# A fixed order of operations on four engines for a top-k attention and SoLU kernel, with two scratch buffers for its counting passes

## The chip, the cores and the metric

The kernel runs on one core of a Trainium2 chip. A core has a matrix engine (PE, whose weight loads are listed as PEld), a vector engine (DVE), a scalar engine (ACT), a general engine (POOL) and a synchronisation engine (SP, used here for DMA). Each takes its instructions from its own queue in order; semaphores let one wait for another. The metric is the device time of one execution in microseconds.

## The reference

Attention keeps, in each row of scores, the 32 largest; what follows is a feed-forward block whose activation is SoLU with a layer norm. All is float32 in the result; the weights come in as float64.

```python
# q, k, v: (8, 8, 576, 64) = batch, heads, sequence, head_dim; top_k = 32
scores = scale * np.matmul(q, k.transpose(0, 1, 3, 2))
kth = np.partition(scores, -top_k, axis=-1)[..., -top_k:-top_k + 1]
scores = np.where(scores >= kth, scores, -1000000000.0)
scores = scores - np.max(scores, axis=-1, keepdims=True)
attn = np.exp(scores)
attn = attn / (np.sum(attn, axis=-1, keepdims=True) + 1e-09)
x = np.matmul(attn, v)                 # then (B, H, S, D) -> (4608 tokens, 512)
...
h = x @ w_in                           # 512 -> 1024
e = np.exp(h - h_max)
solu = h * (e / (np.sum(e, axis=-1, keepdims=True) + 1e-09))
ln = (solu - mu) / np.sqrt(var + 1e-06) * g_ln
return (ln @ w_out).astype(np.float32) # 1024 -> 512
```

## The kernel before, in words

The attention works on 32 pairs of heads (8 batches, 4 pairs each). A pair has nine tiles of 128 rows by 576 scores: four tiles of 128 rows for each of two heads, and one that holds the last 64 rows of both. The k-th value of a row isn't found by sorting but by counting and correcting a threshold. For a pair `i` the steps are, by function:

- `load_qk`, `load_v`: DMAs on SP. q and k have one buffer each.
- `prep`: PE transposes q and k into PSUM tiles of the tag `tp` (two of them), ACT copies them; PE makes moments of k and multiplies q with them; DVE (L669, L673) and POOL (L675, L678, a power; L691) turn that into a first threshold `t0` and its step (`ta`, `tb`).
- `scores(i, t)`: for t = 0 to 4, PE writes two score tiles (PSUM tag `big`, two of two banks each; L715). ACT copies each to SBUF (`X`, L723). DVE counts the scores over `t0` (L728); what it writes besides the count goes to a scratch tile `junkv` with one buffer.
- `second`: four short DVE passes (L736 to L743) make the second threshold `t1`.
- `count1`: ACT counts with Sign (L751), scratch `junka` with one buffer. `third`: DVE makes the third threshold `t2` (L760 to L768). `count2`: ACT counts again (L783) and keeps the signs `sg` (nine buffers).
- `nearest`: DVE makes distances to the threshold (`side`'s pass L795, then L801 for each tile) and takes the eight smallest (L805, MAX8). `kth`: seven short DVE passes (L818 to L833) pick the k-th value.
- `exps`: ACT's exponentials of three tiles at a time (L812).
- `softmax`: DVE masks the exponentials and sums them (L843); POOL inverts three sums at a time (L849, and a power, L852) and multiplies the three tiles (L855).
- `transpose_p`, `transpose_last`: PE transposes the probabilities into the `tp` tiles (L872, L890, L886), ACT copies them out (L879, L892, L887). `attn_v`: PE multiplies them with v in three parts (L912), ACT copies the result (L918, L920).

When the four pairs of a batch are done, its tokens are queued in groups of 128: four for a batch, and one more for every second batch, 36 in all. `mm1` (PE, L933), `solu_ln` (DVE L943 to L954, ACT L946 and L958, POOL L959 to L964) and `mm2` (eight transposes L974, copies L977, 16 matmuls L980, copy L985, store from ACT's DMA queue L987). Weights are converted from float64 in 16 chunks (`weights_step`, lines 31 to 52, on DVE and POOL).

The Python code calls these functions from `slot(i)`, which mixes the first half of pair `i` with the second half of pair `i - 1`; `pop()` takes the next piece of token or weight work from a list. This order is a priority only: the framework's scheduler, with its own model of costs, decides in which order each engine gets the instructions, and interleaves them freely where data and buffers allow.

Of the kernel before, what the change touches and what calls it, by code (L numbers as in the profile page):

```python
# [443 lines left out]
def fast_path(  # L444
# [165 lines left out]
    def prep(i):  # L610

        d = st[i]
        qkT = p2.tile([P, 2, S], F32, tag="qkT", name="qkT")

        mom = p2.tile([P, D + 1], F32, tag="mom", name="mom")
        tails = ps_tp.tile([P, NM, P], F32, tag="tp", name="tp_t")
        for n, nm in enumerate("qk"):
            nc.tensor.transpose(
                tails[:, 0, n * ST : (n + 1) * ST], d[nm + "t"].rearrange("p h d -> p (h d)"),
                ident[0:ST, 0:ST],  # L620
            )
        nc.scalar.copy(
            out=qkT[:, :, SM:S],
            in_=tails[:, 0, 0 : 2 * ST].rearrange("p (n s) -> p n s", n=2),
        )
        for n, nm in enumerate("qk"):
            tp = ps_tp.tile([P, NM, P], F32, tag="tp", name="tp_qk")
            for c in range(NM):
                nc.tensor.transpose(
                    tp[:, c, :], d[nm][:, 2 * c : 2 * c + 2, :].rearrange("p h d -> p (h d)"),  # L630
                    ident,
                )
            if nm == "q":
                nc.scalar.copy(out=qkT[:, n, 0:SM], in_=tp.rearrange("p c s -> p (c s)"))
            else:
                nc.scalar.activation(
                    out=qkT[:, n, 0:SM], in_=tp.rearrange("p c s -> p (c s)"), func=AF.Copy,
                    accum_out=mom[:, D : D + 1],
                )
        d["qkT"] = qkT  # L640
        tm = ps_tp.tile([P, NM * P], F32, tag="tp", name="tp_m")
        for c in range(NM + 1):
# [6 lines left out]
        nc.scalar.copy(out=mom[:, 0:D], in_=tm[:, 0:D])  # L649

        ty = ps_tp.tile([P, NM * P], F32, tag="tp", name="tp_y")
        tt = ps_o.tile([P, 512], F32, tag="o", name="y_t")
        ys = [
            ty[:, 0 : NM * (D + 1)].rearrange("p (t e) -> p t e", e=D + 1),
            tm[:, 2 * D : 2 * D + NM * (D + 1)].rearrange("p (t e) -> p t e", e=D + 1),
            tt[:, 0 : D + 1].unsqueeze(1),
        ]
        for t in range(NM + 1):
            for h in range(2):
                hd = slice(h * D, (h + 1) * D)  # L660
                qs = slice(SM, S) if t == NM else slice(t * P, (t + 1) * P)
                nc.tensor.matmul(
                    out=ys[2][h * ST : (h + 1) * ST, 0, :] if t == NM else ys[h][:, t, :],
                    lhsT=trunc(qkT[hd, 0, qs]), rhs=trunc(mom[hd, :]), start=True, stop=True,
                )
        ys = [(slice(h, 2 * NM, 2), ys[h]) for h in range(2)] + [(slice(2 * NM, NT), ys[2])]
        yq = p2.tile([P, NT, D], F32, tag="w", name="yq")
        for js, y in ys:
            nc.vector.tensor_tensor(  # L669
                out=yq[:, js, :], in0=y[:, :, 0:D], in1=d["q"][:, js, :], op=ALU.mult  # L670
            )
        ss = small.tile([P, NT], F32, tag="ss", name="ss")
        nc.vector.tensor_reduce(out=ss, in_=yq, axis=AX.X, op=ALU.add)  # L673
        zs = small.tile([P, NT], F32, tag="zs", name="zs")
        nc.gpsimd.tensor_scalar(  # L675
            out=zs, in0=ss, scalar1=(Z0 * scale) ** 2 / S, scalar2=0.0, op0=ALU.mult, op1=ALU.add
        )
        nc.gpsimd.tensor_tensor(out=zs, in0=zs, in1=phalf.broadcast_to([P, NT]), op=ALU.pow)  # L678
        t0 = small.tile([P, NT], F32, tag="t0", name="t0")
        for js, y in ys:  # L680
            nc.vector.scalar_tensor_tensor(
                out=t0[:, js], in0=y[:, :, D], scalar=scale / SM, in1=zs[:, js],
                op0=ALU.mult, op1=ALU.add,
            )

        ta = small.tile([P, NT], F32, tag="ta", name="ta")
        nc.vector.scalar_tensor_tensor(
            out=ta, in0=zs, scalar=GAIN, in1=t0, op0=ALU.mult, op1=ALU.add
        )
        tb = small.tile([P, NT], F32, tag="tb", name="tb")  # L690
        nc.gpsimd.tensor_scalar(  # L691
            out=tb, in0=zs, scalar1=-63.0 * GAIN, scalar2=1.0, op0=ALU.mult, op1=ALU.mult
        )
        d["t0"], d["ta"], d["tb"] = t0, ta, tb
# [4 lines left out]
    def scores(i, t):  # L699
# [19 lines left out]
        for j, s in zip(js, big):  # L719
            if j % 3 == 0:  # L720
                d["X"][j // 3] = p6.tile([P, 3, S], F32, tag="X", name="X")
            x = x_of(i, j)
            nc.scalar.activation(  # L723
                out=x.rearrange("p (a s) -> p a s", a=2), in_=s[:, :, 0:SH],
                func=AF.Copy, scale=scale,
            )
            junk = p1.tile([P, S], BF16, tag="junkv", name="junkv")
            nc.vector.tensor_scalar(  # L728
                out=junk, in0=x, scalar1=d["t0"][:, j : j + 1], scalar2=None,
                op0=ALU.is_ge, op1=ALU.add, accum_out=d["c0"][:, j : j + 1],  # L730
            )
# [16 lines left out]
    def count1(i, j):  # L748
        d = st[i]
        junk = p1.tile([P, S], BF16, tag="junka", name="junka")  # L750
        nc.scalar.activation(  # L751
            out=junk, in_=x_of(i, j), func=AF.Sign, scale=-1.0,
            bias=d["t1"][:, j : j + 1], accum_out=d["n1"][:, j : j + 1],
        )
# [33 lines left out]
    def nearest(i, g):  # L788

# [7 lines left out]
        for j in range(3 * g, 3 * g + 3):  # L799
            w = p2.tile([P, S], F32, tag="w", name="w")  # L800
            nc.vector.scalar_tensor_tensor(  # L801
                out=w, in0=x_of(i, j), scalar=d["al"][:, j : j + 1], in1=d.pop(("sg", j)),
                op0=ALU.subtract, op1=ALU.mult,
            )
            nc.vector.max(d["w8"][:, j, :], w)  # L805
# [33 lines left out]
    def softmax(i, g):  # L839
        d = st[i]  # L840
        for j in range(3 * g, 3 * g + 3):
            e = d["E"][g][:, j % 3, :]
            nc.vector.scalar_tensor_tensor(  # L843
                out=e, in0=x_of(i, j), scalar=d["kth"][:, j : j + 1], in1=e,
                op0=ALU.is_ge, op1=ALU.mult, accum_out=den_all[:, i, j : j + 1],
            )
        js = slice(3 * g, 3 * g + 3)
        rden = d["rden"][:, js]
# [4 lines left out]
        for j in range(3 * g, 3 * g + 3):  # L853
            e = d["E"][g][:, j % 3, :]
            nc.gpsimd.tensor_scalar(  # L855
                out=e, in0=e, scalar1=d["rden"][:, j : j + 1], scalar2=1.0,
                op0=ALU.mult, op1=ALU.mult,
            )
# [4 lines left out]
    def transpose_p(i, j):  # L863
        d = st[i]
# [4 lines left out]
        pt = p_of(i, j)  # L869
        tp = ps_tp.tile([P, NM, P], F32, tag="tp", name="tp_p")  # L870
        for c in range(NM):
            nc.tensor.transpose(tp[:, c, :], pt[:, c * P : (c + 1) * P], ident)  # L872
# [6 lines left out]
        nc.scalar.copy(out=dst, in_=tp)  # L879

    def transpose_last(i, part):

        d = st[i]
        tp = ps_tp.tile([P, NM, P], F32, tag="tp", name="tp_pt")
        if part == 2:
            nc.tensor.transpose(tp[0:ST, 0, :], p_of(i, 2 * NM)[:, SM:S], ident)  # L886
            nc.scalar.copy(out=d["PTt"][0:ST, NM, :], in_=tp[0:ST, 0, :])  # L887
            return
        for n in range(4):
            nc.tensor.transpose(tp[0:ST, n, :], p_of(i, 4 * part + n)[:, SM:S], ident)  # L890
# [3 lines left out]
    def attn_v(i, part):  # L894
# [13 lines left out]
        for c in range(NM + 1):  # L908
            ks = P if c < NM else ST
            for h in range(2):  # L910
# [5 lines left out]
                )  # L916
        if part == 1:
            nc.scalar.copy(out=xs["m", b][:, hp, :], in_=d["om"])  # L918
        elif part == 2:
            nc.scalar.copy(  # L920
                out=xs["t", b // 2][:, hp, (b % 2) * ST : (b % 2 + 1) * ST], in_=o
            )
            d.clear()
            if hp == NP - 1:
                queue_batch(b)
# [3 lines left out]
    def mm1(d, x):  # L929
# [10 lines left out]
    def solu_ln(d):  # L940
        h = d["h"]
        nmax = small.tile([P, 1], F32, tag="hmax", name="hmax")
        nc.vector.tensor_reduce(out=nmax, in_=h, axis=AX.X, op=ALU.max, negate=True)  # L943
        e = p1.tile([P, DFF], F32, tag="e", name="e_sb")
        rs = small.tile([P, 1], F32, tag="rs", name="rs")
        nc.scalar.activation(out=e, in_=h, func=AF.Exp, bias=nmax, accum_out=rs)  # L946
        nc.vector.tensor_scalar(out=rs, in0=rs, scalar1=1e-9, scalar2=None, op0=ALU.add)
        nc.vector.reciprocal(rs, rs)
        solu = p2.tile([P, DFF], F32, tag="solu", name="solu")
        nmu = small.tile([P, 1], F32, tag="nmu", name="nmu")  # L950
        nc.vector.scalar_tensor_tensor(
            out=solu, in0=h, scalar=rs, in1=e, op0=ALU.mult, op1=ALU.mult, accum_out=nmu
# [4 lines left out]
        var = small.tile([P, 1], F32, tag="var", name="var")  # L957
        nc.scalar.activation(out=e, in_=solu, func=AF.Square, bias=nmu, accum_out=var)  # L958
# [6 lines left out]
            out=solu, in0=solu, scalar1=nmu, scalar2=rstd, op0=ALU.add, op1=ALU.mult  # L965
        )
        d["ln"] = solu

    def mm2(d, stores):
# [42 lines left out]
    def pop():  # L1012
        if todo:
            todo.pop(0)()
# [116 lines left out]
```

## Time and profile before

| | |
|---|---|
| median of 3 runs | 1764.85 us (1764.52 to 1766.37) |
| the profiled execution | 1766.6 us, span 1764.7 us |
| mean granted PE clock | 0.864 |
| POOL `softmax` waiting for DVE's L843 | 467.6 us in 53 waits |
| ACT `count1` waiting for DVE's `second` | 126.1 us in 32 waits |
| DVE `third` waiting for ACT's `count1` | 134.2 us in 20 waits |

The span runs from the first to the last instruction of the profiled execution. In a group's or timeline's row stand the engine, the line, the operation, the tile written and the tiles read, the shapes and the number of instructions; busy time is given in microseconds. PEclk is the clock that PE was granted, as a share of full speed.

### The profile page before, as it was taken

What the parts mean: (1) busy time and instruction counts of PE and PEld (TensorE: products, weight loads), DVE (VectorE), ACT (ScalarE), POOL (GpSimd) and SP (SyncE); (2) the same over time, 40 slices, a digit from 0 to 9 for tenths busy, and PEclk for the clock granted to TensorE, in tenths of its full rate; (3) what the DMA queues carried; (4) which work ended last, traced back from release to release, by engine and by line L of the source; (5) the groups of instructions that cost most, each with busy time, mean ns of one, the idle gap of its engine ahead of it and who ended that gap; (6) DMA issues with size and microseconds to landing.
All of it is one profiled execution on the core that took longest, in us unless ns stands there. A gap on an engine that the chain in (4) does not pass through costs nothing.

```text
span 1764.7 us, 21722 instructions
## 1 busy us (share of the span) xinstructions
PE 1423.9 (81%) x7043; PEld 782.8 (44%) x7043; DVE 1155.7 (65%) x2816; ACT 1175.2 (67%) x2398; POOL 647.3 (37%) x806
## 2 busy tenths in 40 slices
PE   5364478998889897998789988798789988799696
PEld 3232244454444454544444554445435445345443
DVE  3687876687757567666766677576766856567520
ACT  3656587677866767678767767667776768676521
POOL 5778623342324333142243331333233412433210
PEclk9576688898889888898789988898888988899898
DMA  3211100011001110101101010011001110100000
GB/s 98 73 50 51 33 22 21 21 27 35 14 21 33 28 28 7 27 27 28 26 24 27 20 29 21 21 28 33 22 12 29 28 26 22 27 13 20 1 12 20
DMA packets 101898, 48.68 MB, mean 28 GB/s; under 512 B 86920, under 2 KB 95120, under 8 KB 101776
## 3 DMA queue, kind: packets, MB, share of 16 engines
q1 hardware_dynamic: 96528, 37.77, 8.4%
q10 hardware_dynamic: 5248, 9.44, 1.5%
q8 instruction: 58, 0.95, 0.2%
q14 instruction: 64, 0.52, 0.1%
HBM read 37.75 MB, written 9.44 MB: 27 GB/s over the span
## 4 chain that ended last, share of the span: by engine, by line
PE 38%; DVE 22%; ACT 16%; POOL 15%; issue 7%; DMA 1%; SPq 0%; ACTq 0%; DVEq 0%; POOLq 0%
PE o_ps L980 9%; PE om L912 8%; PE tp_p L872 8%; PE s_ps L715 7%; ACT junka L751 7%; DVE junkv L728 5%; DVE E L843 5%; POOL zs L678 3%; ACT sg L783 3%; DVE w L801 3%; POOL E L855 3%; DVE w L805 2%; POOL solu L964 2%; PE tp_pt L890 2%; PE tp_ln L974 2%
## 5 line engine op out<-in xcount | busy, mean ns | idle before, releaser
L715 PE MATMUL s_ps<-qkT 64*128 64x288 f32 (+1 forms) x1280 | 335.8, 483 | 70.6 <-ACT X L723 50.0
L751 ACT ACTIVATE junka<-X,t 128x576 bf16<-128x576 f32 x288 | 223.0, 774 | 131.2 <-DVE t L743 126.1
L872 PE MATMUL tp_p<-ident,E 128*128 128x128 f32 x1152 | 206.6, 330 | 117.9 <-POOL E L855 59.7
L728 DVE TENSOR_SCALAR_CACHE_REDUCE junkv<-X,t 128x576 bf16<-128x576 f32 x288 | 232.3, 807 | 85.3 <-ACT X L723 78.0
L980 PE MATMUL o_ps<-w_out,lnT 128*128 128x512 f32 x576 | 264.9, 612 | 0.0
L843 DVE SCALAR_TENSOR_TENSOR E<-X,kth,E 128x576 f32<-128x576 f32 x288 | 250.5, 898 | 15.9 <-ACT E L812 13.3
L872 PEld LDWEIGHTS tp_p<-ident,E 128*128 128x128 f32 x1152 | 156.7, 168 | 209.3 <-issue 96.2
L855 POOL TENSOR_SCALAR E<-E,rden 128x576 f32<-128x576 f32 x288 | 243.7, 860 | 9.8
L879 ACT COPY PT<-tp_p 128x512 f32<-128x512 f32 x256 | 143.1, 587 | 151.6 <-PE tp_p L872 149.0
L933 PE MATMUL h_ps<-w_in,xTm 128*128 128x512 f32 x512 | 232.1, 597 | 0.6 <-ACT xTm L918 0.6
L783 ACT ACTIVATE sg<-X,t 128x576 bf16<-128x576 f32 x288 | 220.4, 772 | 16.5 <-DVE t L768 16.2
L715 PEld LDWEIGHTS s_ps<-qkT 64*128 64x128 f32 (+1 forms) x1280 | 161.1, 195 | 157.9 <-ACT X L723 80.7
L801 DVE SCALAR_TENSOR_TENSOR w<-X,al,sg 128x576 f32<-128x576 f32 x288 | 229.5, 823 | 0.6
L849 POOL TENSOR_SCALAR rden<-den_all 128x3 f32<-128x3 f32 x96 | 30.9, 322 | 542.0 <-DVE E L843 467.6
L723 ACT ACTIVATE X<-s_ps 128x576 f32<-128x576 f32 x288 | 178.4, 650 | 68.9 <-PE s_ps L715 56.6
L805 DVE MAX8 w<-w 128x8 f32<-128x576 f32 x288 | 209.8, 750 | 0.0
L980 PEld LDWEIGHTS o_ps<-w_out,lnT 128*128 128x128 f32 x576 | 110.4, 197 | 133.7 <-issue 126.3
L812 ACT ACTIVATE E<-X 128x1728 f32<-128x1728 f32 x96 | 157.6, 1647 | 12.2 <-PE tp_pt L890 12.1
L912 PE MATMUL om<-PT,vm 128*64 128x256 f32 x1024 | 161.7, 454 | 0.1
L933 PEld LDWEIGHTS h_ps<-w_in,xTm 128*128 128x128 f32 x512 | 93.2, 190 | 103.8 <-issue 98.7
L912 PEld LDWEIGHTS om<-PT,vm 128*64 128x64 f32 x1024 | 89.3, 165 | 59.2 <-issue 39.0
L974 PE MATMUL tp_ln<-ident,solu 128*128 128x128 f32 x288 | 52.4, 317 | 63.0 <-POOL solu L964 63.0
(119 smaller groups left out, 1632.0 us busy)
## 6 DMA issues: line engine op xcount, KB each, us to landing
qm<-in_q_dram SPq DMA_DIRECT2D x32, 256.0 KB, 3.4
km<-in_k_dram SPq DMA_DIRECT2D x32, 256.0 KB, 3.3
vm<-in_v_dram SPq DMA_DIRECT2D x32, 256.0 KB, 2.8
out_dram<-osb ACTq DMA_DIRECT2D x32, 256.0 KB, 2.3
w_raw<-in_moe_w_in_dram SPq DMA_DIRECT2D x8, 512.0 KB, 3.8
w_raw<-in_moe_w_out_dram SPq DMA_DIRECT2D x8, 512.0 KB, 3.5
qt<-in_q_dram SPq DMA_DIRECT2D x32, 32.0 KB, 2.2
kt<-in_k_dram SPq DMA_DIRECT2D x32, 32.0 KB, 2.8
```

What stands on the lines that cost most here:

```text
L715: nc.tensor.matmul(out=s[:, half, 0:SH], lhsT=qkT[hd, 0, qs], rhs=qkT[hd, 1, half * SH : (half + 1) * SH], start=True, stop=True,)
L728: nc.vector.tensor_scalar(out=junk, in0=x, scalar1=d["t0"][:, j : j + 1], scalar2=None, op0=ALU.is_ge, op1=ALU.add, accum_out=d["c0"][:, j ...
L751: nc.scalar.activation(out=junk, in_=x_of(i, j), func=AF.Sign, scale=-1.0, bias=d["t1"][:, j : j + 1], accum_out=d["n1"][:, j : j + 1],)
L783: nc.scalar.activation(out=d["sg", j], in_=x_of(i, j), func=AF.Sign, scale=-(1.0 + 2.0**-23), bias=d["t2"][:, j : j + 1], accum_out=d["n2" ...
L801: nc.vector.scalar_tensor_tensor(out=w, in0=x_of(i, j), scalar=d["al"][:, j : j + 1], in1=d.pop(("sg", j)), op0=ALU.subtract, op1=ALU.mult,)
L805: nc.vector.max(d["w8"][:, j, :], w)
L843: nc.vector.scalar_tensor_tensor(out=e, in0=x_of(i, j), scalar=d["kth"][:, j : j + 1], in1=e, op0=ALU.is_ge, op1=ALU.mult, accum_out=den_a ...
L855: nc.gpsimd.tensor_scalar(out=e, in0=e, scalar1=d["rden"][:, j : j + 1], scalar2=1.0, op0=ALU.mult, op1=ALU.mult,)
L872: nc.tensor.transpose(tp[:, c, :], pt[:, c * P : (c + 1) * P], ident)
L912: nc.tensor.matmul(out=o[h * D : (h + 1) * D, :], lhsT=vm[:, h, c, :] if c < NM else vt[:, h, :], rhs=rhs[0:ks, c, :], start=(c == 0), sto ...
L933: nc.tensor.matmul(out=h[:, half, :], lhsT=x[:, c, :], rhs=w_in[:, c, half * 512 : (half + 1) * 512], start=(c == 0), stop=(c == NP - 1),)
L980: nc.tensor.matmul(out=o, lhsT=lnT[:, c, :], rhs=w_out[:, c, :], start=(c == 0), stop=(c == NF - 1),)
```

## The change

Every function is cut at its changes of engine, so that each piece issues instructions to one engine (for a few, two). Each piece gets a time within a step of 40 us per pair, from a table written by hand (`pair_times`, `token_times`); all pieces are sorted by time and issued in that order inside a block that fixes the order of PE, ACT, DVE and POOL to the order of the code. SP's order is still the scheduler's. A pair's second half has the times of the step after its first; token groups have one step each (the last five 15 us each, behind the last pair), the extra groups half a step.

Besides: `junkv` and `junka` get two buffers; the products with the moments go to one `big` tile and one `o` tile and take two DVE passes where there were three, and the mean is scaled in its own pass before the power is ready; stores go out from SP's queue. The arithmetic is otherwise the same.

```diff
-    def prep(i):
+    def prep_t(i):        # two transposes of the tails
...
+    def prep_tc(i):       # ACT's copy of them
...
+    def prep_m(i, nm):    # four transposes of q or k
...
+    def prep_mc(i, nm):   # ACT's copy
...
+    def moments(i):       # PE;   moments_c: ACT's copy
...
+    def spread(i):
+        y = ps_big.tile([P, 2, 512], F32, tag="big", name="y_ps")
...
+    def spread_v(i):      # DVE: per part one product and one scaled mean
...
+    def spread_r(i):
+        nc.vector.tensor_reduce(out=d["ss"], in_=d["yq"], axis=AX.X, op=ALU.add)
+    def first_p(i):       # POOL: scale, power, tb
...
+    def first(i):
+        nc.vector.tensor_tensor(out=d["t0"], in0=d["mean"], in1=d["zs"], op=ALU.add)
...
+    def evac(i, j):       # ACT's copy of one score tile
...
+    def count0(i, j):
-            junk = p1.tile([P, S], BF16, tag="junkv", name="junkv")
+        junk = p2.tile([P, S], BF16, tag="junkv", name="junkv")
...
     def count1(i, j):
         d = st[i]
-        junk = p1.tile([P, S], BF16, tag="junka", name="junka")
+        junk = p2.tile([P, S], BF16, tag="junka", name="junka")
...
-    def nearest(i, g):
+    def side(i, g):       # the pass on three tiles' thresholds
...
+    def nearest(i, j):
+        w = p2.tile([P, S], F32, tag="w", name="w")
+        nc.vector.scalar_tensor_tensor(
+            out=w, in0=x_of(i, j), scalar=d["al"][:, j : j + 1], in1=d.pop(("sg", j)),
+            op0=ALU.subtract, op1=ALU.mult,
+        )
+        nc.vector.max(d["w8"][:, j, :], w)
...
-    def softmax(i, g):
+    def keep(i, j):       # DVE, one tile
...
+    def inverse(i, g):    # POOL, three sums
...
+    def norm(i, j):       # POOL, one tile
...
+    # copy_p, copy_last, copy_v: ACT's copies of transpose_p, transpose_last, attn_v
+    # hmax, hexp, solu, square, ln, transpose_ln, copy_ln, mm2, store: the token pieces
...
-            nc.scalar.dma_start(out=dst, in_=osb[rows, :])
+            nc.sync.dma_start(out=dst, in_=osb[rows, :])
...
+    STEP = 40.0
+    def at(time, f, *args):
+        todo.append((time, len(todo), f, args))
+    def pair_times(i):
+        b = i * STEP
+        if i == 0:
+            at(b - 40, load_qk, 0)
+        else:
+            at(b - 30, load_qk, i)
+        at(b + 1, load_v, i)
+        at(b - 18.0, prep_t, i)
+        at(b - 17.4, prep_m, i, "q")
+        at(b - 13.9, prep_tc, i)
+        at(b - 13.6, prep_mc, i, "q")
+        at(b - 13.5, prep_m, i, "k")
+        at(b - 13.0, prep_mc, i, "k")
+        at(b - 12.9, moments, i)
+        at(b - 12.4, moments_c, i)
+        at(b - 12.2, spread, i)
+        at(b - 9.6, spread_v, i)
+        at(b - 8.8, spread_r, i)
+        at(b - 5.0, first_p, i)
+        at(b - 2.5, first, i)
+        for t in range(NM + 1):
+            at(b - 2.6 + 1.75 * t, scores, i, t)
+        for j in range(NT):
+            at(b - 1.3 + 0.875 * j, evac, i, j)
+            at(b - 0.6 + 0.875 * j, count0, i, j)
+            at(b + 9.0 + 0.78 * j, count1, i, j)
+            at(b + 19.9 + 0.78 * j + (1.5 if j > 3 else 0), count2, i, j)
+        at(b + 7.4, second, i)
+        at(b + 16.6, third, i)
+        b += STEP
+        for g, t in enumerate((7.4, 16.8, 18.3)):
+            at(b + t, exps, i, g)
+            at(b + 8.35 + 4.35 * g, side, i, g)
+            at(b + 26.0 + 2.6 * g, inverse, i, g)
+        at(b + 21.5, kth, i)
+        for j in range(NT):
+            at(b + 8.4 + 1.45 * j, nearest, i, j)
+            at(b + 23.0 + 0.8 * j, keep, i, j)
+            at(b + 27.0 + 0.78 * j + 0.2 * (j // 3), norm, i, j)
+            at(b + 28.0 + 0.85 * j, transpose_p, i, j)
+            at(b + 28.7 + 0.85 * j, copy_p, i, j)
+        for part, t in enumerate((31.2, 34.6, 35.4)):
+            at(b + t, transpose_last, i, part)
+            at(b + t + 0.6, copy_last, i, part)
+            at(b + t + 1.2, attn_v, i, part)
+        at(b + 38.0, copy_v, i, 1)
+        at(b + 39.0, copy_v, i, 2)
+    def token_times(n, x, stores):
+        d = {"x": x, "stores": stores}
+        late = n > NPAIR
+        b = (NPAIR + 1) * STEP + 15.0 * (n - NPAIR - 1) if late else n * STEP
+        c = b + 15.0 if late else b + STEP
+        at(b + 6.5, mm1, d)
+        at(b + 13.9, hmax, d)
+        at(b + 15.8, hexp, d)
+        at(b + 17.2, solu, d)
+        at(b + 22.2, square, d)
+        at(b + 23.6, ln, d)
+        for g in range(2):
+            at(c + (13.7 if late else 5.7) + 0.3 * g, transpose_ln, d, g)
+            at(c + (13.8 if late else 6.4) + 0.4 * g, copy_ln, d, g)
+        at(c + 14.3, mm2, d)
+        at(c + 21.5, store, d)
...
+    at(-11.0, load_g)
+    at(-14.0, load_w, 0)
     for n in range(len(w_chunks) + 2):
-        todo.append(lambda n=n: weights_step(n))
-    for i in range(NPAIR + 1):
-        slot(i)
-    while todo:
-        pop()
+        at(11.0 + 9.7 * n, weights_step, n)
...
+    E = mybir.EngineType
+    with tc.manual_schedule(engines={E.PE, E.Activation, E.DVE, E.Pool}):
+        for _, _, f, args in sorted(todo, key=lambda x: x[:2]):
+            f(*args)
```

The `+` lines with a comment stand for functions whose passes are those of the functions before.

## The prediction

> **What bounds the kernel now.** I read the page first: the share of busy time, the granted clock and the chain.
>
> ```profile
> span 1764.7 us, 21722 instructions
> ...
> PE 1423.9 (81%) x7043; PEld 782.8 (44%) x7043; DVE 1155.7 (65%) x2816; ACT 1175.2 (67%) x2398; POOL 647.3 (37%) x806
> ...
> PEclk9576688898889888898789988898888988899898
> ...
> PE 38%; DVE 22%; ACT 16%; POOL 15%; issue 7%; DMA 1%; SPq 0%; ACTq 0%; DVEq 0%; POOLq 0%
> ```
>
> No engine is full and the chain hops between four of them, so what counts is how well one pair's work hides another's. The timeline of DVE gives the period: the row of `second` (L741) in pair 14 and in pair 22.
>
> ```profile
> 749.93 0.16 DVE L741 TENSOR_TENSOR u<-r,tb 128x9 f32<-128x9 f32 x1
> ...
> 1159.53 0.16 DVE L741 TENSOR_TENSOR u<-r,tb 128x9 f32<-128x9 f32 x1
> ```
>
> Eight pairs take 409.6 us, so 51.2 us a pair. The engines' own work is much less: ACT 1175.2/32 = 36.7, DVE 36.1, PE 44.5 with its half-clock stretches in it. A perfect order could save 14 us a pair. The fixed order must be judged by the longest chain that its in-order queues close.
>
> The scores, ACT and PE timelines at full clock:
>
> ```profile
> 717.50 1.19 ACT L723 ACTIVATE X<-s_ps 128x576 f32<-128x576 f32 x2 [0.51 <-PE s_ps L715]
> 719.48 1.19 ACT L723 ACTIVATE X<-s_ps 128x576 f32<-128x576 f32 x2 [0.78 <-PE s_ps L715]
> ```
> ```profile
> 718.21 1.77 PE L715 MATMUL s_ps<-qkT 64*128 64x288 f32 x8 [0.27 <-ACT X L723]
> ```
>
> With two score tiles, PE waits for ACT's copies and ACT for PE: a group of two takes 1.98 us, and the first copy comes 1.27 after its matmuls start. Today the scheduler puts other pairs' transposes into these holes.
>
> The end of a pair's softmax, POOL timeline:
>
> ```profile
> 746.17 0.20 POOL L849 TENSOR_SCALAR rden<-den_all 128x3 f32<-128x3 f32 x1 [24.37 <-DVE E L843]
> ...
> 747.42 3.21 POOL L855 TENSOR_SCALAR E<-E,rden 128x576 f32<-128x576 f32 x3
> ...
> 752.86 2.18 POOL L855 TENSOR_SCALAR E<-E,rden 128x576 f32<-128x576 f32 x3
> ...
> 756.37 2.18 POOL L855 TENSOR_SCALAR E<-E,rden 128x576 f32<-128x576 f32 x3
> ```
>
> Three groups take 746.17 to 758.55 = 12.4 us. The first three products take 3.21, not 2.18, because DVE runs its own two-operand passes (L843) meanwhile, and these slow from 0.81 to 1.23:
>
> ```profile
> 750.01 1.22 DVE L843 SCALAR_TENSOR_TENSOR E<-X,kth,E 128x576 f32<-128x576 f32 x1
> ...
> 751.25 0.81 DVE L843 SCALAR_TENSOR_TENSOR E<-X,kth,E 128x576 f32<-128x576 f32 x1
> ```
>
> Single scratch, DVE timeline at the start: counts back to back start 0.94 apart for 0.81 of work.
>
> ```profile
> 29.48 0.81 DVE L728 TENSOR_SCALAR_CACHE_REDUCE junkv<-X,t 128x576 bf16<-128x576 f32 x1
> ...
> 30.42 0.81 DVE L728 TENSOR_SCALAR_CACHE_REDUCE junkv<-X,t 128x576 bf16<-128x576 f32 x1
> ```
>
> The clock, by windows (stretch, its length, PE's busy time, ...; the third number from the end is the granted clock):
>
> ```profile
> 707.50:721.10 13.60, 11.90 (x60) 6.21 (x58) 3.91 (x12) 10.95 (x27) 3.67 (x5) 1.00 0.25 65
> 721.20:731.40 10.20, 9.64 (x36) 6.05 (x38) 9.86 (x22) 4.45 (x6) 0.52 (x2) 0.50 0.01 2
> 731.40:741.60 10.20, 10.20 (x87) 5.96 (x84) 6.57 (x13) 7.67 (x12) 0.00 (x0) 1.00 0.00 0
> ```
>
> After a stretch of bare scores with PE half idle the clock halves, and stays there through 10.2 us of nearly full PE.
>
> **The change, part by part.** *Two scratch buffers.* ACT's counts (L751) start 0.90 apart today, those of L783, which have nine buffers, 0.76: 9 x 0.14 = 1.3 us of ACT a pair. DVE: up to 0.21 x 9 = 1.9, but in the new order a count waits for its score copy (0.99 apart on average), so nothing there. ACT's 36.7 becomes 35.4, which binds nothing below.
>
> *Small edits*, at nothing: the moments' products are regrouped (three passes of 0.34, 0.33, 0.13 and three of 0.07 become about the same), inside DVE's wait for the next scores; if that cover went, 0.2 us a pair. Stores move from ACT's queue to SP's: 40 issues of some 0.34 us leave ACT; on SP a load may queue behind one (0.6 each), but loads stand at 10.0 of the step and are needed at 22.0, and land in 3.4. Without that cover, 3 to 7 us a pair.
>
> *The order.* Sorted by the table, and since each engine runs in order, one step closes this loop: scores of pair i+1, then their counts and `second`, then on DVE (behind `second`) `nearest` and `kth` of pair i, `keep`, POOL's `inverse` and `norm`, PE's transposes and `attn_v` of pair i, and only behind these, on PE, scores of pair i+2. Priced at full clock:
>
> - scores to `second`: 1.27 + 4 x 1.98 + the last copy 0.65 + the last count 0.89 + `second`, which alone on DVE takes 1.25 (1623.93 to 1625.18): 12.0.
> - DVE to `kth`: `nearest` puts MAX8 (0.66 apart) directly behind the pass that it reads. The trace never does: it pairs them (two L801, then two L805), 0.73 apart. Bounds 0.73 to 0.94 (the scratch wait above); I take 0.84, duration plus 0.03, as L825 to L828 (dependent) show. 9 x 1.50 = 13.5. `side` 3 x 0.2, `hmax` 1.2, `third` 0.5, `solu` 1.7, `kth` 1.7 (L818 to L843). Sum 19.2.
> - three `keep` and the step to POOL: 2.4.
> - POOL: 12.4 as above, since six `keep` are left when it starts, as at 746. Bounds: 3 x 3.42 = 10.3 with none in the way, 3 x 4.5 = 13.5.
> - PE behind the last `norm`: three blocks of transposes through two PSUM tiles, with copies 1.4, `attn_v` 2.4 (736.77 to 739.30) and 0.95: 4.75.
>
> Sum 50.7. Other waits in the loop end early: DVE comes to `hmax` at 18.1 (12.0 + side + four `nearest`) when `mm1` ended at 16.8; ACT runs copies, `exps`, nine counts and reaches `count2` at 23.6, after `third` at 22.7; pair i+1's prep is done on PE and ACT by 33, before the first `norm`. The table's own distance for this loop is 40: it gives nine `nearest` 13.1 us with no room for `hmax`, `third` and `solu` among them, and 2.6 per POOL group.
>
> The clock comes on top. PE ends the token matmuls about 23.4 after the scores began (8.7 for four groups and the last one's 0.76, 0.9 for eight transposes, and twice 6.9, the length of 16 matmuls of L980 at full clock) and gets the first `norm` at 35.6, with 3 us of `prep` between: half clock when transposes begin. At half clock `attn_v` takes 3.7 (3.08 at 729.06 and 0.65) for 2.4, a transpose starts 213 ns behind the last instead of 109, and a score group, whose matmuls grow by 0.96, would take 2.9. Bounds 0 (all hidden under POOL) to 5 (all of the tail, and two score groups at 2.9). I take 1.5, since `attn_v` part 0 stands before the last four transposes and the row above shows the clock back after 10 us of dense work. Step: 52.2.
>
> The Trainium skill ("TensorE: Matmul & The Clock Gate", Part 1) has full clock back after one busy window of about 3.4 us; by it the addition would be about 1.0, where the row at 721.2 needed three such windows. "SBUF — State Buffer" (the shared port pair) says that a DVE pass with two SBUF inputs and a POOL pass exclude each other entirely; by it three products would take 4.4, not the 3.21 of the row, and the step 1.2 more.
>
> *Start.* `second` of pair 0 as today, 44. Step 0: three weight conversions of 6.7 us on POOL stand before `first_p`, which today slips between them: 31 (today 22). Steps 1 to 3 lack `hmax` and `solu` (-2.9), have two conversions' DVE work (2 x 1.9) and one POOL conversion between the `norm` groups (+6.7): 3 x 59.8. Step 4: 53.1. `second` of pair 5 at 308; today 275.5.
>
> *Middle.* 26 steps x 52.2 = 1357, against today's 1349 (1624.8 - 275.5). Three extra token groups at half steps put 6.9 us of `mm2` between transposes: 3 x 5.
>
> *End*, from `second` of pair 31: pair 30's DVE work 27.4, pair 31's `nearest` to three 6.3, a wait for the last `mm1` until 48.5, then 1.2 + 11.3 + 2.4 + 12.4 + 4.75 = 80.6; five late groups, 11 bursts of 6.9 and six changes of 1.5: 84.6, store 3: about 170. Today 139.9: there the groups mix with the last pair.
>
> Sum: 308 + 1357 + 15 + 170 = 1850. The profiled run took 1766.6 for its span of 1764.7, and the median is 1764.85, so span and median agree within 0.2: 1850.
>
> **The rivals.** *Faster: the loop at its lower ends.* `nearest` at 1.40 (12.6), `side` 0.3, `second` 0.87, POOL 10.3, PE tail 3.5, no clock loss: 11.6 + 17.9 + 2.3 + 10.3 + 3.5 = 45.6, and 1625 in all (start 273, middle 1186 + 9, end 155); halfway, a step of 48, 1725. For it: ACT's and DVE's work would allow 37. Against: POOL's 12.4 is measured with the same neighbours. It decides below a step of 49, where the middle's gain of 75 pays for start and end. Chance 0.28.
>
> *Slower still: the clock.* If PE stays at half through tail and scores, 50.7 + 5 = 55.7, and 1955. For it, bare scores halved the clock at 721; against, `attn_v` fills a window before them. Chance 0.17.
>
> *No difference*: gain in the middle equals start and end. 0.03 for within 0.2%, about what a measurement of this kernel can tell.
>
> **How the numbers follow.** The forecast (step 49.2 to 54, 1770 to 1910) has 0.52. Below 1670 (step under 46.7) and above 1920 I leave about one in ten each. Faster 0.28 (the lower-end case), same 0.03, slower 0.52 + 0.17 = 0.69.
>
> **What would show it.** Right: `second` repeats every 52 us; DVE is idle over 10 us a step between `spread_r` and the next counts; POOL's `inverse` waits on `keep`; the first score matmul follows `attn_v` directly; half clock between the token matmuls and `attn_v`. Wrong: a step under 49, DVE or ACT over 75% busy in the middle, MAX8 0.73 behind its pass, or full clock throughout.

## The result and the profile after

| | before | after |
|---|---|---|
| median | 1764.68 us (4 runs) | 1995.17 us (4 runs, 1994.64 to 1995.56) |
| ratio | | 1.1306, 95% interval 1.1287 to 1.1326 |
| profiled execution's span | 1764.7 us | 1993.4 us |
| mean granted PE clock | 0.864 | 0.831 |

The kernel became 230 us slower, where 85 were forecast and the range ended at 1920. The page after, span, busy time, granted clock and chain:

```profile
span 1993.4 us, 21797 instructions
...
PE 1426.5 (72%) x7043; PEld 793.5 (40%) x7043; DVE 1219.6 (61%) x2784; ACT 1178.4 (59%) x2398; POOL 659.3 (33%) x806
...
PEclk9986577788878898888887888788888888888899
...
DVE 40%; PE 37%; ACT 10%; POOL 5%; issue 5%; DMA 2%; SPq 0%; DVEq 0%; POOLq 0%; ACTq 0%
```

Work is nearly unchanged (PE 1423.9 before, ACT 1175.2; DVE 1155.7, so 64 us less than after); its shares fell. The chain is now DVE and PE in turn, 77% together, where before it hopped between four engines. The DVE timeline, three repeats of `second`, and how `nearest` runs:

```profile
555.55 0.17 DVE L779 TENSOR_TENSOR u<-r,tb 128x9 f32<-128x9 f32 x1
...
610.67 0.17 DVE L779 TENSOR_TENSOR u<-r,tb 128x9 f32<-128x9 f32 x1
...
611.15 0.82 DVE L842 SCALAR_TENSOR_TENSOR w<-X,al,sg 128x576 f32<-128x576 f32 x1
612.00 0.76 DVE L846 MAX8 w<-w 128x8 f32<-128x576 f32 x1
612.68 0.80 DVE L842 SCALAR_TENSOR_TENSOR w<-X,al,sg 128x576 f32<-128x576 f32 x1
...
628.57 1.04 DVE L859 TENSOR_SCALAR far<-n 128x9 f32<-128x9 f32 x1
...
631.06 0.82 DVE L883 SCALAR_TENSOR_TENSOR E<-X,kth,E 128x576 f32<-128x576 f32 x1
...
648.61 0.17 DVE L722 TENSOR_TENSOR t<-mean,zs 128x9 f32<-128x9 f32 x1 [8.25 <-POOL zs L712]
...
665.53 0.17 DVE L779 TENSOR_TENSOR u<-r,tb 128x9 f32<-128x9 f32 x1
```

55.1 and 54.9 us a step. A MAX8 starts 0.85 after its pass, and a tile takes 1.53. The POOL timeline of the same step, `inverse` and `norm`, then `first_p` (L708 to L714):

```profile
633.45 0.70 POOL L891 TENSOR_SCALAR rden<-den_all 128x3 f32<-128x3 f32 x1 [3.86 <-DVE E L883]
634.23 1.31 POOL L894 TENSOR_TENSOR rden<-rden,minus 128x3 f32<-128x3 f32 x1
635.65 3.73 POOL L898 TENSOR_SCALAR E<-E,rden 128x576 f32<-128x576 f32 x3
...
644.21 2.19 POOL L898 TENSOR_SCALAR E<-E,rden 128x576 f32<-128x576 f32 x3
646.48 0.21 POOL L708 TENSOR_SCALAR zs<-ss 128x9 f32<-128x9 f32 x1
```

And PE's timeline from the transposes to the next scores:

```profile
636.99 3.56 PE L909 MATMUL tp_p<-ident,E 128*128 128x128 f32 x12 [4.20 <-POOL E L898]
641.50 1.11 PE L909 MATMUL tp_p<-ident,E 128*128 128x128 f32 x4 [0.95 <-POOL E L898]
642.41 1.06 PE L929 MATMUL tp_pt<-ident,E 128*64 128x128 f32 x4
643.38 1.94 PE L909 MATMUL tp_p<-ident,E 128*128 128x128 f32 x8
645.25 2.00 PE L958 MATMUL om<-PT,vm 128*64 128x256 f32 x16
...
647.76 1.09 PE L909 MATMUL tp_p<-ident,E 128*128 128x128 f32 x8
...
650.61 1.95 PE L958 MATMUL om<-PT,vm 128*64 128x256 f32 x16
...
653.95 1.24 PE L747 MATMUL s_ps<-qkT 64*128 64x288 f32 x8
```

The last `norm` ends at 646.40. PE is then in `attn_v(0)` (645.25), with the transposes of the last three tiles, `attn_v(1)` and `attn_v(2)` behind it. Scores follow at 653.95, 7.55 after the last `norm`. The chain of the step, followed back from the end, comes to PE from the `norm` of the fourth tile, not from the last, and stays on PE (and ACT's copies) until the scores; in it `om` with 20 matmuls is `attn_v(0)`:

```profile
640.70 0.76 POOL E L898
...
641.50 1.11 PE tp_p L909 x4
...
645.32 2.51 PE om L958 x20
...
654.02 1.16 PE s_ps L747 x7
```

The windows of PE in that step (the third number from the end is the granted clock):

```profile
624.00:637.00 13.00, 2.44 (x27) 1.62 (x25) 12.62 (x30) 8.86 (x24) 5.71 (x7) 0.67 0.17 47
636.90:641.40 4.50, 3.34 (x12) 2.14 (x12) 3.46 (x9) 1.76 (x3) 4.24 (x6) 0.50 0.06 13
641.40:645.20 3.80, 3.70 (x16) 2.82 (x16) 0.00 (x0) 1.75 (x3) 3.53 (x7) 0.50 0.28 64
645.20:654.00 8.80, 8.47 (x80) 5.08 (x79) 0.34 (x2) 3.56 (x7) 3.42 (x5) 0.99 0.00 0
```

So the loop that the prediction drew is there, in its order: the fixed queues close it once a step. It accounts at most for what the steps lost. Of the 229 us by which the span grew, 126 lie between `second` of pair 5 and of pair 31, 58 before and 45 behind; no run was made for the start or the end by itself. What had to be found out is whether it is the cause of the loss, and why it is longer than 52.2.

### The profile page after: what moved, and what is told of

The parts are those of the page before. It is cut to its first block, busy times and chain, and to the rows that moved or that the text cites. A ratio compares the mean times of both kernels' runs of the same rounds, so it can differ in the third digit from the quotient of the medians.

```text
span 1993.4 us, 21797 instructions
## 1 busy us (share of the span) xinstructions
PE 1426.5 (72%) x7043; PEld 793.5 (40%) x7043; DVE 1219.6 (61%) x2784; ACT 1178.4 (59%) x2398; POOL 659.3 (33%) x806
## 4 chain that ended last, share of the span: by engine, by line
DVE 40%; PE 37%; ACT 10%; POOL 5%; issue 5%; DMA 2%; SPq 0%; DVEq 0%; POOLq 0%; ACTq 0%
PE s_ps L747 11%; DVE w L842 10%; DVE w L846 10%; DVE E L883 9%; PE om L958 8%; PE tp_p L909 6%; ACT X L758 5%; PE h_ps L982 3%; PE o_ps L1046 3%; PE tp_pt L929 3%; POOL E L898 2%; DVE hmax L991 2%; DVE solu L1006 2%; POOL rden L894 1%; PE ot L958 1%
## 5 line engine op out<-in xcount | busy, mean ns | idle before, releaser
L909 PE MATMUL tp_p<-ident,E 128*128 128x128 f32 x1152 | 248.8, 369 | 207.0 <-POOL E L898 200.6
L747 PE MATMUL s_ps<-qkT 64*128 64x288 f32 (+1 forms) x1280 | 293.2, 493 | 44.4 <-ACT X L758 43.6
L909 PEld LDWEIGHTS tp_p<-ident,E 128*128 128x128 f32 x1152 | 172.6, 186 | 280.1 <-POOL E L898 247.4
L814 POOL TENSOR_SCALAR tt<-t 128x9 f32<-128x9 f32 x32 | 7.5, 233 | 781.2 <-DVE al L830 778.7
L898 POOL TENSOR_SCALAR E<-E,rden 128x576 f32<-128x576 f32 x288 | 260.0, 920 | 9.7
L1046 PE MATMUL o_ps<-w_out,lnT 128*128 128x512 f32 x576 | 254.9, 595 | 1.0 <-ACT lnT L1041 1.0
L846 DVE MAX8 w<-w 128x8 f32<-128x576 f32 x288 | 219.2, 761 | 9.9
L747 PEld LDWEIGHTS s_ps<-qkT 64*128 64x128 f32 (+1 forms) x1280 | 151.5, 199 | 168.2 <-ACT X L758 139.1
L633 PE MATMUL tp_qk<-ident,km 128*128 128x128 f32 x128 | 35.6, 434 | 254.4 <-ACT qkT L623 254.4
L958 PE MATMUL om<-PT,vm 128*64 128x256 f32 x1024 | 132.3, 403 | 0.0
```

What stands on the lines that cost most here:

```text
L747: nc.tensor.matmul(out=s[:, half, 0:SH], lhsT=qkT[hd, 0, qs], rhs=qkT[hd, 1, half * SH : (half + 1) * SH], start=True, stop=True,)
L898: nc.gpsimd.tensor_scalar(out=e, in0=e, scalar1=st[i]["rden"][:, j : j + 1], scalar2=1.0, op0=ALU.mult, op1=ALU.mult,)
L909: nc.tensor.transpose(tp[:, c, :], p_of(i, j)[:, c * P : (c + 1) * P], ident)
L958: nc.tensor.matmul(out=o[h * D : (h + 1) * D, :], lhsT=vm[:, h, c, :] if c < NM else vt[:, h, :], rhs=rhs[0:ks, c, :], start=(c == 0), sto ...
L1046: nc.tensor.matmul(out=d["o"], lhsT=d["lnT"][:, c, :], rhs=w_out[:, c, :], start=(c == 0), stop=(c == NF - 1),)
```

## The experiments

The loop theory says: the step is as long as the chain scores, `count0`, `second`, `nearest`, `kth`, `keep`, `norm`, transposes, `attn_v`, next scores; the four engines' work doesn't matter. Its rivals: a fixed order costs by itself (signals between engines, the scheduler's freedom gone), or the buffers, or the clock.

**The scratch buffers, each way round.** The kernel before with two of each:

```diff
-            junk = p1.tile([P, S], BF16, tag="junkv", name="junkv")
+            junk = p2.tile([P, S], BF16, tag="junkv", name="junkv")
...
-        junk = p1.tile([P, S], BF16, tag="junka", name="junka")
+        junk = p2.tile([P, S], BF16, tag="junka", name="junka")
```

> The kernel before with the two scratch buffers alone. Theory (the fixed order closes one loop per pair: scores, DVE, POOL, PE, scores): the buffers take 1.3 us a pair off ACT and up to 1.9 off DVE, which are 67% and 65% busy, so 1735 to 1770 us. Rival (the buffers are what costs, for instance by moving the scheduler's choices): over 1850 us.

1777.3 us, ratio 1.0068 (1.0051 to 1.0085): outside the range of the theory by 7 us, and far below the rival's. The 0.14 that each of ACT's counts should gain is gained (0.76 apart instead of 0.90), but the scheduler places operations by priority as they come free, and arranged them otherwise: 52.13 a pair in the middle instead of 51.9, and 5 us more before pair 5. The changed kernel with one buffer each:

> The changed kernel with one scratch buffer each, as before. Theory: in the fixed order a DVE count waits 0.4 to 0.6 us for ACT's copy of its scores anyway, and ACT's nine counts lie beside the DVE part of the loop, so 1990 to 2010 us. Rival (the counts stand in the loop and the second buffer saves 0.14 to 0.21 us on each): 2040 us or more.

2001.3 us, ratio 1.1335 (1.1316 to 1.1354). In the fixed order the buffers bring 6 us at most: the intervals of the two ratios overlap.

**The order left free.** The cut pieces and the table stay, the block that fixes the four queues goes:

```diff
-    with tc.manual_schedule(engines={E.PE, E.Activation, E.DVE, E.Pool}):
+    with ExitStack():
```

> The changed kernel with everything as it is, but the block that fixes the order taken away: the scheduler orders the four engines again, with the table as priority only. Theory: the loss of 230 us comes from the fixed order, so 1700 to 1810 us. Rival (the cut functions, the regrouped products, the stores from SP or the table itself cost it): over 1900 us.

1850.1 us, ratio 1.0478 (1.0457 to 1.0499). Fixing costs 145 of the 230; 85 remain with the order free, and the result lies between the two ranges. The 145 are hardly in the regular step, which took 54.5 to 54.6 us here too: 50 come off before `second` of pair 5, 50 between pairs 5 and 31 (mostly in the longer steps), 43 at the end. Given the pieces in this table's order, the scheduler also put 34 of a pair's 40 score matmuls behind `attn_v` on PE in most steps. So the long step comes with these pieces and this table, whether the order is fixed or not. What part of the 85 is due to the table, and what to the cut functions, the regrouped products or the stores, is left open.

**Scores earlier.** The first half of a pair 8.5 units earlier, with the three extra token groups moved too:

```diff
-        b = i * STEP
+        b = i * STEP - LEAD      # LEAD = 8.5: preparation, scores, count0, second
```

> The changed kernel with the first half of each pair (prep, scores, copies, first counts, second) 8.5 us earlier in the table, so that the scores of pair i+2 stand among the transposes of pair i on PE and not behind attn_v; the extra token groups move to 7 us behind the group of their step, because their PSUM tile would block the scores. Theory: the loop is opened, DVE's own work (35 to 37 us) becomes the bound, and the step falls from 54.9 to 40 to 46 us: 1560 to 1760 us in all. Rival (many small waits and the half clock, no single loop): the step stays over 51 us, over 1880 us.

1958.0 us, ratio 1.1089 (1.1067 to 1.1111): a miss for the loop theory. PE's timeline tells why:

```profile
623.07 0.22 PE L674 MATMUL y_t<-mom,qkT 64*64 64x65 bf16 x2
638.14 1.97 PE L909 MATMUL tp_p<-ident,E 128*128 128x128 f32 x8 [14.85 <-POOL E L898]
640.03 2.29 PE L747 MATMUL s_ps<-qkT 64*128 64x288 f32 x8
```

Two transposes (places 28.0 and 28.85) still stood ahead of the first scores (28.9). PE waited 14.85 us for the first `norm` with ready scores behind. The loop wasn't opened, only closed through another `norm`: 54.4 a step. Two transposes in front were enough.

**The tail later.** Now the places were worked out first: each operation's measured duration laid in the order of the table, each engine in order, an operation starting when its engine, its inputs and its buffers are free. For the changed kernel that sum gives 54.8 a step. Then the PE tail alone was moved:

```diff
-            at(b + 28.0 + 0.85 * j, transpose_p, i, j)
+            at(b + TAIL + 28.0 + 0.85 * j, transpose_p, i, j)   # TAIL = 8.5
```

and the same for `copy_p`, `transpose_last`, `copy_last`, `attn_v` and `copy_v`.

> The changed kernel with the transposes, their copies and attn_v of a pair given places 8.5 units later in the table, so that on TensorE the first scores of the next pair stand between them and no longer behind all of them; nothing else moves. Loop theory (the step is as long as the closed chain scores, count0, second, nearest, kth, keep, norm, transposes, attn_v, scores): laying the durations that the trace of the changed kernel shows in the order of its table gives 54.8 us a step (54.87 were measured); in the new order the same sum gives 49.5, because the chain now closes through the normalizations and the small POOL pass that count0 needs, not through attn_v. Expected step 49 to 51.5, total 1835 to 1905. Rival (fixing the order costs what it costs through signals between engines or the TensorE clock, wherever the tail stands): step 54 to 56, total 1970 to 2020.

1852.7 us, ratio 1.0496 (1.0479 to 1.0514), regular steps of 49.1 to 51.3. 142 us come off by moving one family in an order that stays fixed.

**All places.** The table's other numbers were then chosen by the same sum, over many sets of places:

```diff
-            at(b - 2.6 + 1.75 * t, scores, i, t)            # b = i * STEP
+            at(c + -6.791 + 1.789 * t, scores, i, t)        # c = i * STEP
...
-            at(b + 19.9 + 0.78 * j + (1.5 if j > 3 else 0), count2, i, j)
+            at(c + 30.664 + 0.734 * j + (3.863 if j > 3 else 0), count2, i, j)
...
-            at(b + 8.4 + 1.45 * j, nearest, i, j)           # b = (i + 1) * STEP
+            at(c + 33.647 + 2.315 * j, nearest, i, j)       # 14.8 earlier
...
-            at(b + 28.0 + 0.85 * j, transpose_p, i, j)
+            at(c + 74.454 + 0.86 * j, transpose_p, i, j)    # 6.5 later
...
```

> The same pieces as the changed kernel, the same four engines in a fixed order, but every piece of a pair's step has another place, chosen so that by the durations measured in the changed kernel no chain closes on itself in one step: nearest starts a good ten units earlier and runs among the count2 passes, scores and count0 come some four units earlier, transposes and attn_v six to nine later, the preparation four to nine earlier. Loop theory: the same sum gives 41 us a regular step and 435 us less than for the changed kernel in all; the changed kernel measured 100 more than its own sum, so 1480 to 1620 is expected, with VectorE's own work (about 38 us a step) the next bound. Rival (a fixed order loses by itself, whatever the places): no less than the 1850 that the same pieces took with the order left free.

1556.3 us (1553.4 to 1557.8), ratio 0.8812 (0.8798 to 0.8827): 439 us faster than the changed kernel and 12% faster than the one before, with the same pieces, the same fixing and the same buffers. Its page:

```profile
span 1553.7 us, 21673 instructions
...
PE 1304.7 (84%) x7043; PEld 726.4 (47%) x7043; DVE 1219.2 (78%) x2784; ACT 1145.8 (74%) x2398; POOL 703.4 (45%) x806
...
PEclk8566667899999999999999999999999999998898
...
POOL 25%; PE 24%; DVE 24%; ACT 18%; issue 6%; DMA 3%; SPq 0%; POOLq 0%; DVEq 0%; ACTq 0%
```

The chain is spread over four engines again. PE's busy time fell by 122 us with the higher clock; that is less than the 439 won, so the clock can't be the whole gain. DVE's timeline shows the new order, counts of the next pair among `nearest` of this one; in these rows nothing waits:

```profile
704.88 0.80 DVE L766 TENSOR_SCALAR_CACHE_REDUCE junkv<-X,t 128x576 bf16<-128x576 f32 x1
705.61 0.81 DVE L842 SCALAR_TENSOR_TENSOR w<-X,al,sg 128x576 f32<-128x576 f32 x1
706.45 0.76 DVE L846 MAX8 w<-w 128x8 f32<-128x576 f32 x1
707.13 0.80 DVE L766 TENSOR_SCALAR_CACHE_REDUCE junkv<-X,t 128x576 bf16<-128x576 f32 x1
```

A step of 40.0 us in the window after, with PE busy for 37.0 of it at full clock and DVE (the third busy time) for 36.5. Both are near the bound, and which of them sets the 40.0 is not shown:

```profile
709.96:749.96 40.00, 37.03 (x219) 20.79 (x218) 36.46 (x85) 35.03 (x74) 18.52 (x22) 1.00 0.12 31
```

**One family back.** In that kernel `nearest`, `side` and `kth` get the changed kernel's places again, after `second`:

```diff
-            at(c + 33.647 + 2.315 * j, nearest, i, j)
+            at(c + 48.4 + 1.45 * j, nearest, i, j)
```

> The kernel of e11_all_places with one family put back: nearest, its sides and kth stand where the changed kernel has them, in one block after second. Loop theory: VectorE's 20 us from second to kth come back into the chain that keep, norm and the transposes close; by the same sum 46 us a regular step instead of 41 (40.0 measured in e11_all_places), total 1690 to 1760. Rival (in the new order VectorE's busy time is the bound, and its order among its own passes costs nothing): 1550 to 1580.

1757.7 us, ratio 0.9962 (0.9948 to 0.9976), regular steps of 46.2 to 46.9: 201 us for the place of one block on DVE.

**Which term was short.** `attn_v(0)` multiplies only two of its five blocks of keys:

```diff
-        for c in range(NM + 1):
+        for c in (0, NM) if part == 0 else range(NM + 1):
```

> The changed kernel with attn_v(0) multiplying only the first and the last of its five blocks of keys (12 of its 20 matmuls left out, 2.65 us shortened by some 1.6). The prediction reckoned the TensorE end of a step from the last norm: transposes of the last tile, attn_v(1) and attn_v(2), 4.75 us, with attn_v(0) under the norms. If that was right, attn_v(0) is covered and the time stays: 1985 to 2000. If instead TensorE works without a gap from the fourth transpose to the first scores, so that attn_v(0) lies in the chain (7.55 us measured from the last norm), 1.6 us times 31 steps come off: 1935 to 1960.

1939.5 us, ratio 1.0998 (1.0979 to 1.1016): 56 us off, so `attn_v(0)` lies in the chain.

```profile
624.33 1.11 PE L909 MATMUL tp_p<-ident,E 128*128 128x128 f32 x4 [0.95 <-POOL E L898]
...
628.08 1.12 PE L958 MATMUL om<-PT,vm 128*64 128x256 f32 x4
629.13 1.05 PE L958 MATMUL om<-PT,vt 64*64 64x256 f32 x4
...
636.31 1.24 PE L747 MATMUL s_ps<-qkT 64*128 64x288 f32 x8
```

From the fourth transposes to the scores it takes 11.98 us (12.45 in the changed kernel). In such a regular step only 0.5 to 0.8 is won and not 1.6, since the eight matmuls left take up to 2.1 at a clock of 0.50 to 0.74 (the twenty took 2.5 to 2.8 at 0.88 to 1.00). The rest of the 56 came off before pair 5 (12), in the steps around the extra groups (17) and from the steps of 57, which shrank to 52 to 55; so the total in the range is partly luck. In three of those without an extra group the clock stayed up through the whole stretch. The eight matmuls took 1.16 there, the stretch 9.81, the scores came 4.9 behind the last `norm` (1018.15 in the row shown), and the step fell to 52.22:

```profile
1013.24:1023.05 9.81, 9.34 (x81) 5.78 (x81) 0.34 (x2) 5.21 (x10) 6.86 (x10) 1.00 0.12 26
```

**The clock.** Nine more matmuls a step, repeats of `mm2` into its tile after the copy, in PE's empty stretch:

```diff
+            at(c + 22.65, fill, d, 5)
+            at(c + 27.9, fill, d, 4)
```

> The changed kernel with nine matmuls a step more, repeats into a tile whose sum was already copied out, placed in the stretch in which TensorE otherwise idles between mm2 and the transposes, so that the granted clock does not fall there; the output is unchanged. Clock theory: the tail from the last norm to the first scores shrinks from 7.55 us to about 5.5 and the steps of 57 us with scores at half clock vanish; total 1915 to 1960. Rival (TensorE is not late at full clock either, it waits for the norms and copies): 1985 to 2005, the clock up but the time unchanged.

1995.6 us, ratio 1.1298 (1.128 to 1.1317): no change in the total, with the mean clock at 0.908. PE's windows in a step:

```profile
619.90:633.60 13.70, 10.54 (x49) 4.97 (x48) 13.29 (x32) 9.56 (x26) 5.65 (x7) 1.00 0.16 43
633.60:638.10 4.50, 1.97 (x12) 1.26 (x12) 3.43 (x9) 1.76 (x3) 4.24 (x6) 1.00 0.03 7
638.10:641.60 3.50, 3.43 (x18) 2.51 (x18) 0.00 (x0) 1.75 (x3) 3.23 (x6) 0.57 0.35 77
641.60:650.40 8.80, 8.47 (x78) 5.05 (x77) 0.34 (x2) 3.57 (x7) 3.69 (x6) 0.98 0.01 2
```

The first three transposes ran at full clock and then waited for the norms all the same; while they did, PE was busy for 1.97 of 4.50 us, and the clock fell for the next 3.5. The rest of the tail, 8.8 us, is as long as in the changed kernel, where it was already at 0.99. A regular step took 54.65. In two steps of this run the clock did stay up through the whole tail (from 308.44 and from 871.05). From the fourth transposes to the scores it took 11.1 us there, 6.20 of them behind the last `norm` (which ended at 875.95 in the second), and the second of these steps took 53.45:

```profile
871.05:882.15 11.10, 10.44 (x93) 6.65 (x93) 0.34 (x2) 5.12 (x10) 6.86 (x10) 1.00 0.09 21
```

So the half clock costs 1.35 us of the 7.55 in the changed kernel's regular step. The matmuls that were added did not remove it from the other steps, and the end of the run became 7.5 us longer.

**Two small ones.** `nearest` split, so that a MAX8 needn't follow its own pass:

> The changed kernel with nearest split in two, subtract-multiply and MAX8, and two of the first kind issued ahead of the two maxima in each group of three, so that a MAX8 follows its pass 0.73 us and not 0.84 behind. Loop theory: nearest lies in the closed chain, so 6 to 9 times 0.1 us a step come off: total 1965 to 1985. Rival (VectorE idles 15 us a step, so nothing that makes it shorter shows): 1990 to 2000.

1974.7 us, ratio 1.1184 (1.1166 to 1.1203): in range, but not as expected. DVE's stretch from `second` to the first `keep` is 0.8 shorter, yet a regular step only 0.25; 7 of the 20 us come off before pair 5, most of the rest from the steps of 57. The other 0.6 of the 0.8 is lost on PE: from the fourth transposes to the scores it takes 13.06 us instead of 12.45, because the clock, at 0.50 for 3.80 us, is still at 0.79 in the next 3.10, with PE busy all the time:

```profile
633.90:637.00 3.10, 3.10 (x22) 1.53 (x21) 0.00 (x0) 0.58 (x1) 2.93 (x4) 0.79 0.00 0
```

The extra token groups 13 units earlier:

> The changed kernel with the three extra token groups given places 13 units earlier in the step, ahead of scores and not in the middle of nearest. The steps around an extra group now take 58.9 and 63.0 us against 54.9. Loop theory: part of the group still lies in the chain, by the same sum 7 of the 12.2 us stay: total 1975 to 1988. Rival (an extra group costs its work wherever it stands): 1990 to 2000.

1971.1 us, ratio 1.1174 (1.1155 to 1.1193), a little better than expected. An extra group now takes one longer step, 60.1 (54.9 regular), where it took two, 58.9 and 63.0.

**One engine free.** PE's order left to the scheduler, the other three fixed:

> The changed kernel with the order fixed on ScalarE, VectorE and POOL only; TensorE's order is left to the scheduler. If TensorE's fixed order alone closed the chain, this comes near the 1850 that the order free on all engines gave: 1840 to 1880. If the chain closes as well through the others (the evacuations of the scores stand behind the copies of the transposes on ScalarE, first_p behind the norms on POOL), most of it stays: 1930 to 2000.

1986.7 us, ratio 1.1267 (1.1248 to 1.1286). PE's freedom alone is worth 8 us, and not in the step: the start is 8 us shorter and the end 14, while the regular steps are longer, 55.9 to 57.4. Whether the loop closes through ACT and POOL as well, as was expected, is not shown by this, since here too the scheduler put 34 of a pair's 40 score matmuls behind `attn_v` in most steps.

## Why the prediction was partly right, point by point

- *Direction and mechanism.* Right: the kernel became slower, and the loop is what sets the step. Moving places within the same fixed order spans 1556 to 1995 us, and three regular steps came near what the sum of durations had given for the new places (49.5, 41 and 46). What a fixed order costs by itself, if anything, is less than its places can win: 1556. Of the 14 us in "a perfect order could save 14 us a pair" 11.2 came: 40.0 a step stands against 51.2.
- *Scores to `second`, 12.0.* 11.96 measured (599.08 to 611.04).
- *DVE to `kth`, 19.2.* 20.0 (to 631.06); MAX8 behind its pass at 0.85 for 0.84. The 0.8 is in `far` (L859): 1.04 instead of the 0.16 it takes elsewhere, while POOL runs `ln`.
- *`keep` and step to POOL, 2.4.* 2.39.
- *POOL, 12.4.* 12.95 (633.45 to 646.40).
- *PE behind the last `norm`, 4.75 and 1.5 for the clock.* The step that failed: 7.55. The 4.75 was counted from the last `norm`, as if PE had kept up with the ones before. It hadn't: from the fourth transposes at 641.50 PE works 12.45 us almost without a gap, and `attn_v(0)`, reckoned as covered by the norms, stands in the queue before the last three tiles' transposes. At full clock the same end takes 6.20 (the row at 871.05), and 4.9 where 12 of the 20 matmuls of `attn_v(0)` are left out (the row at 1013.24). So 4.75 was right for what it counted, and 1.45 was left out of it. The clock has the other 1.35: it stood at 0.50 from 641.40 to 645.20, inside this stretch. The 1.5 was about right in size.
- *Regular step, 52.2.* The terms give 54.85, 54.87 measured: 26 x 2.67 = 69 us. Of the 2.65 a step, PE's end has 1.3, DVE 0.8 and POOL 0.55.
- *Extra token groups, 15.* They took 12.2, 13.5 and 12.2: 23 more. Four other steps of 57.1 to 57.2 instead of 54.9 add 9; in them the scores ran at half clock (0.79 on the mean of the step, 0.84 to 0.85 in the regular ones).
- *Start, 308.* 333.4. `second` of pair 0 came at 26.1 instead of 44, step 0 took 37.0 instead of 31. Steps 1 to 3 took 72.8, 76.1 and 68.4, not 59.8 each: 38 more. The weight pieces stand in the fixed queues of DVE and POOL and wait for each other there (POOL L50 for DVE L47, 27.3 us in 6 waits, 11.6 the longest). How much of the 38 these waits explain is not shown.
- *End, 170.* 184.7; not looked into.
- Together: 69 + 23 + 9 + 25 + 15 = 141 of the 145 missing. The failed step has 26 x 1.3 = 34 of them; no single term has them all.
- *The rivals.* The lower ends (step 45.6 to 48) didn't come: no term was at its lower end. *Clock worse* came near the size (55.7) for the wrong reason: it has 5 us a step of half clock through tail and scores, and in a regular step 1.35 were measured, in the tail alone.
- *Slips in the sums.* `attn_v` from 736.77 to 739.30 is 2.53, not 2.4; 11 x 6.9 + 6 x 1.5 is 84.9, not 84.6; the lower ends add up to 1623, not 1625. In the forecast they are worth under 4 us.
- *The Trainium skill.* The Trainium skill ("TensorE: Matmul & The Clock Gate", Part 1) has the clock back after one dense window of some 3.4 us. Here it stood at 0.50 through 3.80 us with PE busy for 3.70, and at 0.99 in the next 8.80, which agrees. It does not agree with the row of before at 721.2 (10.20 us at 0.50 with PE busy for 9.64), nor with the row at 633.90 above. The Trainium skill ("SBUF — State Buffer", the shared port pair) has DVE and POOL exclude each other in such passes. Three products took 3.73 beside passes of 0.81 to 1.29, and 2.19 in the later groups; by full exclusion the estimate was 4.4. And the three `keep` at 633.3 to 635.6 kept their 0.81 while POOL's two small passes took 0.70 and 1.31 for 0.20 and 0.86: there it was POOL that became slower.
- *Range.* The step lay inside the cases, between 52.2 and the 55.7 of *Clock worse*. Start, extra groups and end had one value each and no width; they missed 25, 23 and 15 us, all on one side, and the upper end at 1920 had no room for that.

## What to carry to other kernels

A fixed order is judged by the longest chain that its in-order queues close in one step, and one early piece in a queue (two transposes ahead of ready scores) is enough to close it. The same table made as long a step with the order left free (54.5 here), so the table is to be judged before the fixing. Lay measured durations in the written order, buffers included, before trusting the table's own distances, which here said 40 where 54.9 came out; the same sum then finds the places that really give 40. Count the end of a chain from the point at which the engine stops waiting, not from its last input.

## What the runs showed that was not expected

- With the denser order the clock was higher too, with no matmul added: the mean granted clock is 0.925 in the kernel with all places moved (1.00 in the step at 709.96), 0.831 in the changed one. PE's busy time fell from 1426.5 to 1304.7 us with the same 7043 matmuls.
- More matmuls that raised the mean clock (0.831 to 0.908) bought nothing in the total. Only in the steps in which the clock also held through the dense tail was the tail shorter, 11.1 us instead of 12.45.
- Short DVE passes can take up to 1 us beside POOL: `far` 1.04 for the 0.16 that it takes in the kernel with all places moved, a pass of `kth` (L872 in the kernel with `nearest` split) 1.03 for 0.23.
